# Attention with a top-32 cut and a max-out MLP: a first sweep over seven groups of keys, and half of the masks split between VectorE and GpSimd

## The chip, the cores and the metric

The kernel runs on one core of a Trainium2 chip. What counts is the time of one execution on the device in microseconds (us): the median of several runs. Five engines work side by side, each with a queue of its own that is taken in order: TensorE (PE, with its weight loads shown apart as PEld), VectorE (DVE), ScalarE (ACT), GpSimd (POOL) and SyncE (SP), which here issues most of the transfers.

## What is computed

Eight batches of eight heads, 576 tokens, head size 64. Of each row of scores only the 32 largest are kept; the softmax runs over these. The heads' outputs go through an MLP whose hidden layer is the largest of three products. All is float32.

```python
scores = scale * np.matmul(q, k.transpose(0, 1, 3, 2))
kth = np.partition(scores, -top_k, axis=-1)[..., -top_k:-top_k + 1]   # top_k = 32
scores = np.where(scores >= kth, scores, -1000000000.0)
scores = scores - np.max(scores, axis=-1, keepdims=True)
attn = np.exp(scores)
attn = attn / (np.sum(attn, axis=-1, keepdims=True) + 1e-09)
out = np.matmul(attn, v)
...
h = np.maximum(np.maximum(x @ w1, x @ w2), x @ w3)     # x: 4608 x 512, h: 4608 x 768
return h @ w_out
```

## The kernel before

**Tiles and units.** A tile is 128 queries of one head against all 576 keys. A unit is two or four tiles of a pair of heads; 288 tiles in 80 units. For each unit these steps run, and the letters are the names that the program gives to them:

- `q` (PE): scores into PSUM; `e` (ACT, `evac`): evacuation, scaled, into `ssb`.
- `s` (DVE, `sweep`): the first sweep. A MAX8 instruction finds the eight largest of each of eight groups of 72 keys and puts them into `L`.
- `N` (ACT, `negate`), `p1` to `p5` (DVE, `pivot`): from the four largest of each group (`nA`, negated) and the next four, the 24th largest of all of these is found: the pivot, a lower bound. MATCH_REPLACE8 and MAX8 pick the smallest 16 of the 32 negated values, which one instruction compares with the sorted rest.
- `g` (ACT, `sign`): the sign of pivot minus score, and its sum, which tells the pivot's rank. `w` (POOL, `window`): sign times score. `k` (DVE, `below`): a MAX8 over that row gives the eight values under the pivot. `h` 0 to 2 (DVE, `pick`): the 32nd largest, `kth`, from these nine and the rank.
- `m` (DVE, `mask`): one instruction with two tensor inputs turns the scores below `kth` into 1 minus score and the others into minus score, in place, and counts the former into `lost` by its accumulator. Since the scores are tiny (scaled by 2^-61), the exponential that follows makes 0 of the former. `x` (ACT, `expo`): the exponential and its sum.
- `T`, `E` (PE, ACT): transposes and their copies; `v` (PE): the product with the values; `y`, `Y`, `Z` (DVE, ACT, POOL): the result is scaled and split into two f16 halves `xh` and `xl`.

**The MLP.** Per batch there are two spans of tokens, 256 and 320 wide; for each, hidden-layer products on PE (L706, f16, three per pair of halves), evacuation and maximum (ACT L713, DVE L715), a split into halves (ACT L718, POOL L721), and then the second layer (L766) and the output. In the first 200 us the weights are also loaded, decoded on DVE (L253 to L255), scaled and cut into halves.

**What sets the order.** All steps are written down as `Piece`s: an engine, a cost in ns, what it needs and which buffers it takes. `in_order` then plays a list schedule: of each engine's pieces that lie within a window of ranks (`place_of` of the unit plus an entry of the table `OFFSETS`) it takes the first that can start, with a patience per engine, and so writes out each engine's queue before the kernel runs. The MLP's pieces are `fill`: on PE they are taken where no attention piece can start sooner. Pieces marked `alone` (the mask among them) are not put beside a POOL piece: they wait in the schedule for POOL to be free, and POOL's wait for them. On the chip the queues run in that order, and an instruction waits for what it needs.

Of the kernel before, what the change touches and what calls it, by code (L numbers as in the profile page):

```python
# [8 lines left out]
F32 = mybir.dt.float32  # L9
F32R = mybir.dt.float32r  # L10
F16 = mybir.dt.float16
# [9 lines left out]
G = 8  # L21
GW = 72
# [12 lines left out]
LEAD = 122.6  # L35
# [29 lines left out]
def in_order(pieces, fill):  # L65
# [35 lines left out]
    while left:  # L101
# [32 lines left out]
NSM = 2
LOAD_QK = 4000
DECODES = 2
DECODE_IN = 1920.0
DECODE_OUT = 1920.0
LOAD_JOB = 6500
SCORES = 960  # L140
PATIENCE = {'PE': 83.0, 'DVE': 164.4, 'ACT': 0.0, 'POOL': 81.9, 'SP': 0.0}


@with_exitstack
def kernel(ctx, tc, q, k, v, moe_w1, moe_w2, moe_w3, moe_w_out, out):
    nc = tc.nc
    B, NP, _, S = q.shape
    H, D = 2 * NP, q.shape[2] // 2
    P = 128
# [153 lines left out]
    def cut(j, part):  # L303
# [8 lines left out]
        def scaled():  # L312
            down = scale_of[f"w{j}"][0] if j < 3 * NB else scale_of["rows"][:, (j - 3 * NB) * P // CUT:(j - 3 * NB) * P // CUT + 1]
            box["ws"] = io.tile([P, 2 * CUT], F32, name="ws", bufs=2).rearrange("p (c n) -> p c n", n=CUT)
            nc.scalar.activation(box["ws"], w, AF.Copy, scale=down)

        def high():
            nc.scalar.copy(hi, box["ws"])  # L318

        def low():  # L320
            nc.gpsimd.tensor_tensor(lo, box["ws"], hi, ALU.subtract)
        return scaled, high, low

    pieces, fill = [], []
    rings = {nm: Ring(k) for nm, k in dict(s=2, tr=2, m=2, ssb=NSSB, L=NSM, nA=NSM, n8=NSM, nb=3, w=NWB, oh=2, pm=PMB, rs=3, sums=3, den=3,
                                           rsw=2, pT=1, xs=2, junk=2, books=2, vt=6, x=2, h1=3, ob=2, ws=2, qk=3).items()}

    def piece(engine, cost, run, needs=(), rank=(0.0, None), takes=(), mode=None, alone=False):
        x = Piece(engine, cost, run, needs, rank, [(rings[r], rel) for r, rel in takes], mode, alone)
        pieces.append(x)  # L330
        return x

    def scale_pieces(parts_, needs, rank):
        a = piece("DVE", 63, parts_[0], needs, rank)
        rel = []
# [755 lines left out]
```

## Time and profile before

| | before |
|---|---|
| median of 3 runs | 1258.01 us (1257.69 to 1258.57) |
| the profiled execution | 1259.42 us, its span 1257.6 us |
| PE busy | 1146.8 us, 91% |
| DVE busy | 1146.7 us, 91% |
| ACT busy | 1038.8 us, 83% |
| POOL busy | 569.3 us, 45% |

The span is the time from the first to the last instruction of the profiled execution. Busy time counts every moment in which an engine has at least one instruction under way; matmuls overlap in their pipeline and their ends are modelled, so their mean duration is longer than the step from one to the next, and the same holds for short DVE instructions. The view of the slices cuts the span into 40 equal parts of 31.4 us. A view by stretches gives for each engine the busy time and, in brackets, how many instructions started there.

### The profile page before, as it was taken

How to read it: one execution, taken by the hardware profiler on the slowest of the kernel's cores; microseconds unless marked ns; L12 is line 12 of the kernel's file. 1: busy time of each engine (PE TensorE's matmuls, PEld its weight loads, DVE VectorE, ACT ScalarE, POOL GpSimd, SP SyncE). 2: the span in 40 equal slices, each digit the busy share in tenths (PEclk: the TensorE clock that was granted, in tenths of full speed). 3: DMA queues.
4: the chain of work that ended last, by engine and by line, in shares of the span. 5: the costliest groups of instructions: out<-in, count | busy, mean ns of one | idle time of the engine just before them, and what ended most of it. 6: DMA issues, size and time to landing. Idle time of an engine off the chain costs nothing.

```text
span 1257.6 us, 27583 instructions
## 1 busy us (share of the span) xinstructions
PE 1146.8 (91%) x8817; PEld 776.2 (62%) x8817; DVE 1146.7 (91%) x5728; ACT 1038.8 (83%) x2692; POOL 569.3 (45%) x503
## 2 busy tenths in 40 slices
PE   5275886999899999999999999999999999999998
PEld 2142653566576666766676666766677665767765
DVE  7999999999999999999999999999999999997121
ACT  6587888999989988999999989898899989897211
POOL 2444644654345544545555545445535454544111
PEclk8567986999999999999999999999999999999999
DMA  7141121202010102010101102020101000000000
GB/s 246 34 158 39 52 70 49 66 2 80 21 58 18 60 1 76 11 47 31 47 31 39 39 2 85 1 77 2 60 19 60 18 20 26 1 19 2 17 18 29
DMA packets 25754, 54.41 MB, mean 43 GB/s; under 512 B 2688, under 2 KB 2944, under 8 KB 25600
## 3 DMA queue, kind: packets, MB, share of 16 engines
q1 hardware_dynamic: 25296, 52.14, 12.6%
q8 instruction: 71, 1.16, 0.4%
q14 instruction: 83, 0.68, 0.2%
q10 hardware_dynamic: 304, 0.43, 0.1%
HBM read 43.12 MB, written 9.44 MB: 42 GB/s over the span
## 4 chain that ended last, share of the span: by engine, by line
DVE 49%; PE 39%; ACT 7%; issue 3%; POOL 1%; DMA 0%; ACTq 0%; DVEq 0%
PE m L706 19%; DVE L L478 13%; DVE ssb L565 9%; DVE Q L526 8%; PE m L766 5%; PE tr L625 5%; PE tr L650 5%; PE s L461 4%; DVE h L715 3%; DVE nR L502 2%; ACT w L517 2%; ACT pm L574 2%; DVE wall L254 1%; DVE n L504 1%; DVE n L496 1%
## 5 line engine op out<-in xcount | busy, mean ns | idle before, releaser
L522 POOL TENSOR_TENSOR w<-ssb,w 128x576 f32<-128x576 f32 x288 | 414.9, 1460 | 259.3 <-ACT w L517 257.0
L706 PE MATMUL m<-xh,wall 128*128 128x256 f16 (+1 forms) x2304 | 436.5, 287 | 4.8 <-DVE h L715 3.6
L706 PEld LDWEIGHTS <-wall 128*128 128x128 f16 x3456 | 338.0, 98 | 95.4 <-issue 15.9
L478 DVE MAX8 L<-ssb 128x8 f32<-128x72 f32 x2304 | 331.2, 218 | 6.8 <-ACT ssb L469 6.7
L706 PE MATMUL m<-xl,wall 128*128 128x320 f16 (+1 forms) x1152 | 330.7, 287 | 0.0
L574 ACT ACTIVATE pm<-ssb,nb 128x576 f32<-128x576 f32 x288 | 222.7, 775 | 42.4 <-DVE ssb L565 41.7
L565 DVE SCALAR_TENSOR_TENSOR ssb<-ssb,kth 128x576 f32<-128x576 f32 x288 | 241.7, 873 | 2.2
L517 ACT ACTIVATE w<-ssb,Q 128x576 f32<-128x576 f32 x288 | 223.2, 775 | 14.9 <-DVE Q L509 13.5
L633 ACT COPY pT<-tr 128x512 f32<-128x512 f32 (+1 forms) x432 | 215.1, 512 | 12.1 <-PE tr L622 6.6
L526 DVE MAX8 Q<-w 128x8 f32<-128x576 f32 x288 | 212.3, 747 | 1.3 <-POOL w L522 0.8
L625 PE MATMUL tr<-ident,pm 128*128 128x128 f32 x1152 | 183.0, 286 | 33.3 <-ACT pm L574 15.1
L461 PE MATMUL s<-qk 64*128 64x288 f32 (+1 forms) x1280 | 191.1, 451 | 16.6 <-ACT ssb L469 11.1
L469 ACT ACTIVATE ssb<-s 128x576 f32<-128x576 f32 x288 | 184.3, 650 | 10.0 <-PE s L461 9.7
L625 PEld LDWEIGHTS tr<-ident,pm 128*128 128x128 f32 x1152 | 130.2, 144 | 98.5 <-ACT pm L574 39.3
L650 PE MATMUL tr<-pT,vt 128*64 128x256 f32 (+1 forms) x1920 | 183.3, 340 | 0.1
L715 DVE SCALAR_TENSOR_TENSOR h<-m,rises,h 128x256 f32<-128x256 f32 (+1 forms) x192 | 97.2, 506 | 67.4 <-PE m L706 67.3
L650 PEld LDWEIGHTS tr<-pT,vt 128*64 128x64 f32 x1920 | 109.8, 140 | 69.1 <-issue 20.7
L721 POOL TENSOR_TENSOR hl<-h,hh 128x256 f16<-128x256 f32 (+1 forms) x96 | 72.7, 758 | 171.4 <-ACT hh L718 171.3
L461 PEld LDWEIGHTS s<-qk 64*128 64x128 f32 (+1 forms) x1280 | 99.9, 184 | 76.4 <-ACT ssb L469 28.2
L674 POOL TENSOR_TENSOR xl<-xs,xh 128x256 f16<-128x256 f32 (+1 forms) x80 | 55.1, 688 | 196.4 <-ACT xh L670 196.3
L766 PE MATMUL m<-wall,hh 128*128 128x512 f16 (+1 forms) x444 | 130.6, 377 | 3.2 <-ACT wall L318 1.2
L718 ACT CAST hh<-h 128x256 f16<-128x256 f32 (+1 forms) x96 | 41.5, 432 | 54.1 <-DVE h L715 53.4
(95 smaller groups left out, 1148.5 us busy)
## 6 DMA issues: line engine op xcount, KB each, us to landing
vt<-in_v_dram SPq DMA_DIRECT2D x32, 320.0 KB, 3.2
qk<-in_k_dram SPq DMA_DIRECT2D x34, 288.0 KB, 3.0
qk<-in_q_dram SPq DMA_DIRECT2D x33, 288.0 KB, 3.5
wall<-in_moe_w_dram SPq DMA_DIRECT2D x16, 512.0 KB, 6.0
out_dram<-ob SPq DMA_DIRECT2D x32, 256.0 KB, 2.0
wall<-in_moe_w_out_dram SPq DMA_DIRECT2D x3, 512.0 KB, 3.5
ssb<-in_moe_w_out_dram SPq DMA_DIRECT2D x3, 512.0 KB, 3.6
wall<-in_moe_w_dram SPq DMA_DIRECT2D x4, 256.0 KB, 5.9
```

Of the source, the lines that this page charges most:

```text
L461: nc.tensor.matmul(to[:, h, :HALF], both[sl, 0, c0:c0 + m], both[sl, 1, i * HALF:(i + 1) * HALF], start=True, stop=True)
L478: nc.vector.max(d["L"][:, t, k, :], d["ssb"][t][:, k * GW:(k + 1) * GW])
L517: nc.scalar.activation(d["w"][t], d["ssb"][t], AF.Sign, bias=d["Q"][:, t, 0:1], scale=-1.0, accum_out=d["cnt"][:, t:t + 1])
L522: nc.gpsimd.tensor_tensor(d["w"][t], d["ssb"][t], d["w"][t], ALU.mult)
L526: nc.vector.max(d["Q"][:, t, 1:NW], d["w"].pop(t))
L565: nc.vector.scalar_tensor_tensor(ss, ss, d["kth"][:, t:t + 1], ss, ALU.is_lt, ALU.subtract, accum_out=d["lost"][:, t:t + 1])
L574: nc.scalar.activation(d["pm", t // 2][:, t % 2], d["ssb"][t], AF.Exp, bias=d["nb"][:, t:t + 1], scale=-1.0 / SHRINK, accum_out=d["sums"][ ...
L625: nc.tensor.transpose(pt[:, j * P:(j + 1) * P], pm[:, i, 64 * i + j * P:64 * i + (j + 1) * P], ident)
L633: nc.scalar.copy(pT[:, 512 * i:512 * i + m] if i < 2 else pT[:, 8 * P:10 * P], pt[:, :m])
L650: nc.tensor.matmul(to, vt[:, block if i < 4 else 8 + h, :], keys, start=(i == 0), stop=(i == 4))
L706: nc.tensor.matmul(box["ps", i][:, :c1 - c0], a, bb[:, kc, c0:c1], start=(kc == 0 and k == 0), stop=(kc == KC - 1 and k == 2))
L766: nc.tensor.matmul(box["po"][:n, :ds.stop - ds.start], a[:, f, cs], columns_of(bb, ds), start=(f == 0 and k == 0), stop=(f == FC - 1 and k ...
```

## The change

The first sweep is cut into seven groups of 82 or 83 keys: three of them need only the first half of the scores, four the rest. What follows works on 28 values where it had 32, and the pivot is looked up among nine places instead of eight, so that it is again the 24th largest. Of each unit's tiles, numbers 1 and 3 get another mask: a comparison with one tensor input on DVE writes 1 or 0 as f16 into a new tile `under` (three buffers) and counts with the same accumulator; a subtraction on POOL then makes `under` minus score, in place in `ssb`. The exponential of such a tile needs the new POOL piece `M`. The planner's costs for the sweep halves and the masks, two of its patiences, its window of ranks and the whole table `OFFSETS` have new numbers.

```diff
-G = 8
-GW = 72
+G = 7
+EDGES = (0, 82, 164, 247, 329, 412, 494, 576)
+FRONT = 3
...
-LEAD = 122.6
+LEAD = 121.9
...
-OFFSETS = {'C0': -22.23, 'C1': -0.68, 'C2': 16.29, 'C3': 22.05, ...}
+OFFSETS = {'C0': -11.78, 'C1': 1.57, 'C2': 14.49, 'C3': 21.94, ...}
...
+SOFT = (1, 3)
+NM = 3
...
-PATIENCE = {'PE': 83.0, 'DVE': 164.4, 'ACT': 0.0, 'POOL': 81.9, 'SP': 0.0}
+PATIENCE = {'PE': 72.0, 'DVE': 163.8, 'ACT': 0.0, 'POOL': 104.8, 'SP': 0.0}
...
-            for k in range(i * G // 2, (i + 1) * G // 2):
-                nc.vector.max(d["L"][:, t, k, :], d["ssb"][t][:, k * GW:(k + 1) * GW])
+            for k in range(FRONT, G) if i else range(FRONT):
+                nc.vector.max(d["L"][:, t, k, :], d["ssb"][t][:, EDGES[k]:EDGES[k + 1]])
...
-            z = d["z"] = sm.tile([P, 4, 8], F32, name="z", bufs=2)
-            nc.vector.scalar_tensor_tensor(z[:, :nt], d["n8"][:, :nt, 1], -SHRINK, b9s[n % 3][:, :nt, 0:8], ALU.mult, ALU.min)
+            z = d["z"] = sm.tile([P, 4, 9], F32, name="z", bufs=2)
+            low = d["n8"].rearrange("p t a b -> p t (a b)")[:, :nt, 4 * G - 24:4 * G - 15]
+            nc.vector.scalar_tensor_tensor(z[:, :nt], low, -SHRINK, b9s[n % 3][:, :nt], ALU.mult, ALU.min)
...
-        nc.vector.scalar_tensor_tensor(ss, ss, d["kth"][:, t:t + 1], ss, ALU.is_lt, ALU.subtract,
-                                       accum_out=d["lost"][:, t:t + 1])
+        if t in SOFT:
+            m = d["under", t] = wk.tile([P, S], F16, name="under", bufs=NM)
+            nc.vector.tensor_scalar(m, ss, d["kth"][:, t:t + 1], None, ALU.is_lt, ALU.add, accum_out=d["lost"][:, t:t + 1])
+        else:
+            nc.vector.scalar_tensor_tensor(ss, ss, d["kth"][:, t:t + 1], ss, ALU.is_lt, ALU.subtract,
+                                           accum_out=d["lost"][:, t:t + 1])
+
+    def drop(n, t):
+        d = st[n]
+        ss = d["ssb"][t]
+        nc.gpsimd.tensor_tensor(ss, d.pop(("under", t)), ss, ALU.subtract)
...
-                p(("s", g, i), "DVE", 1080, lambda g=g, i=i: sweep(n, g, i),
+                p(("s", g, i), "DVE", 1170 if i else 890, lambda g=g, i=i: sweep(n, g, i),
...
-            p(("m", t), "DVE", 740, lambda t=t: mask(n, t), needs=[d["h", 2]], alone=True)
-            p(("x", t), "ACT", 770, lambda t=t: expo(n, t), needs=[d["m", t], d["p2"]] + ([d["x", t - 1]] if t else [last_x[0]] if last_x else []),
+            if t in SOFT:
+                p(("m", t), "DVE", 530, lambda t=t: mask(n, t), needs=[d["h", 2]], takes=[("under", held(n, "under", t))], alone=True)
+                p(("M", t), "POOL", 1430, lambda t=t: drop(n, t), needs=[d["m", t]])
+                held(n, "under", t).append(d["M", t])
+            else:
+                p(("m", t), "DVE", 800, lambda t=t: mask(n, t), needs=[d["h", 2]], alone=True)
+            p(("x", t), "ACT", 770, lambda t=t: expo(n, t), needs=[d["M" if t in SOFT else "m", t], d["p2"]] + ([d["x", t - 1]] if t else [last_x[0]] if last_x else []),
```

How this moves instructions is shown at three places. In the changed program the lines below the diff's first part stand some 13 further down: L565, the mask, is L573, the soft mask is L571, the subtraction L579, the sweep L481, the hidden-layer products L719.

On PE, just ahead of the first 128x320 product of the hidden layer (first batch, second span), before:

```order
L766 LDWEIGHTS hl
L766 MATMUL m<-wall,hl 128x512
L625 MATMUL tr<-ident,pm 128x128 x4
L461 MATMUL s<-qk 128x288 x4
L706 LDWEIGHTS wall
L706 MATMUL m<-xh,wall 128x320
```

And in the changed program:

```order
L779 LDWEIGHTS hl
L779 MATMUL m<-wall,hl 128x512
L464 MATMUL s<-qk 128x288 x4
L719 LDWEIGHTS wall
L719 MATMUL m<-xh,wall 128x320
```

It is the 680th row of PE's queue in both; one group of four transposes has moved behind this place.

On DVE, ahead of the first step on such a product (the last row of each), before:

```order
L565 SCALAR_TENSOR_TENSOR ssb,lost<-ssb,kth 128x576
L509 TENSOR_REDUCE Q<-z 128x4
L496 MAX n_2845<-nA 128x8 x2
L498 TENSOR_REDUCE nb<-nA 128x2
L502 MATCH_REPLACE nR<-n_2845,nA 128x32 x2
L504 MAX n_2845<-nR 128x8 x2
L478 MAX L<-ssb 128x8 x8
L177 TENSOR_SCALAR e_2887<-s_2883 128x1
L180 TENSOR_SCALAR down_v<-e_2887 128x1
L181 TENSOR_SCALAR back_v<-e_2887 128x1
L715 SCALAR_TENSOR_TENSOR h_2900<-m,rises,h_2831 128x320
```

And in the changed program:

```order
L571 TENSOR_SCALAR under,lost<-ssb,kth 128x576
L541 SCALAR_TENSOR_TENSOR oh<-spots,cnt 128x36
L513 TENSOR_REDUCE Q<-z 128x4
L481 MAX L<-ssb 128x8 x6
L180 TENSOR_SCALAR e_2785<-s_2779 128x1
L183 TENSOR_SCALAR down_v<-e_2785 128x1
L184 TENSOR_SCALAR back_v<-e_2785 128x1
L544 TENSOR_TENSOR oh<-oh,Q 128x36
L546 TENSOR_REDUCE kth<-oh 128x4
L571 TENSOR_SCALAR under,lost<-ssb,kth 128x576
L481 MAX L<-ssb 128x8 x8
L728 SCALAR_TENSOR_TENSOR h_2829<-m,rises,h_2761 128x320
```

Counted over the whole queue up to there: 51 tiles swept and 44 masked before; 50 swept, 20 masked and 21 with the soft mask after. A soft mask is now written ahead of the full masks of its unit.

On POOL, at the start of the fourth batch's MLP (the products of the 256-wide span are split, `hl` 128x256), before:

```order
L721 TENSOR_TENSOR hl<-h_9265,hh 128x256
L522 TENSOR_TENSOR w<-ssb,w 128x576 x4
L721 TENSOR_TENSOR hl<-h_9403,hh 128x256
L674 TENSOR_TENSOR xl<-xs,xh 128x256
L522 TENSOR_TENSOR w<-ssb,w 128x576 x2
L721 TENSOR_TENSOR hl<-h_9547,hh 128x256
```

And in the changed program:

```order
L734 TENSOR_TENSOR hl<-h_9215,hh 128x256
L526 TENSOR_TENSOR w<-ssb,w 128x576 x2
L734 TENSOR_TENSOR hl<-h_9298,hh 128x256
L579 TENSOR_TENSOR ssb<-under,ssb 128x576
L687 TENSOR_TENSOR xl<-xs,xh 128x256
L579 TENSOR_TENSOR ssb<-under,ssb 128x576 x2
L734 TENSOR_TENSOR hl<-h_9459,hh 128x256
```

The subtractions stand between the window products and the splits, in the one queue that POOL has.

## Rows read from the trace of the kernel before

**Rows 1.** The page's busy time of each engine, share of the span, instructions.

```profile
PE 1146.8 (91%) x8817; PEld 776.2 (62%) x8817; DVE 1146.7 (91%) x5728; ACT 1038.8 (83%) x2692; POOL 569.3 (45%) x503
```

**Rows 2.** The page's slices: busy tenths of PE and DVE in 40 equal parts.

```profile
PE   5275886999899999999999999999999999999998
...
DVE  7999999999999999999999999999999999997121
```

**Rows 3.** Busy time by stretches: from:to and length, then each engine, PE's clock, transfers.

```profile
0.00:238.00 238.00, 155.15 (x968) 92.94 (x969) 225.28 (x1018) 183.45 (x436) 109.04 (x92) 0.78 0.28 91
238.00:1163.00 925.00, 902.99 (x7214) 620.98 (x7213) 905.79 (x4677) 837.00 (x2221) 449.48 (x396) 1.00 0.10 33
1163.00:1258.00 95.00, 88.64 (x639) 62.25 (x637) 15.59 (x34) 18.32 (x37) 10.77 (x15) 0.99 0.06 21
```

**Rows 4.** Waits of PE, 0 to 238 us: us in total, times, longest.

```profile
PE tr L622 <- ACT rsw L594: 9.9, 6, 3.5
PE s L461 <- ACT ssb L469: 9.0, 7, 2.8
```

**Rows 5.** Waits of PE, 238 to 1163 us.

```profile
PE tr L625 <- ACT pm L574: 7.4, 19, 0.8
PE tr L625 <- DVE xs L667: 4.5, 6, 1.6
```

**Rows 6.** Stretches, the hidden layer's products (L706) alone: PE, PEld, clock, transfers.

```profile
600.00:650.00 50.00, 19.61 (x154) 14.77 (x153) 1.00 0.15 49
...
1150.00:1200.00 50.00, 36.67 (x302) 29.39 (x301) 1.00 0.03 11
```

**Rows 7.** DVE's groups: xcount | busy us, mean ns | idle before, releaser.

```profile
L565 DVE SCALAR_TENSOR_TENSOR ssb<-ssb,kth 128x576 f32<-128x576 f32 x288 | 241.7, 873 | 2.2
L526 DVE MAX8 Q<-w 128x8 f32<-128x576 f32 x288 | 212.3, 747 | 1.3 <-POOL w L522 0.8
L478 DVE MAX8 L<-ssb 128x8 f32<-128x72 f32 x2304 | 331.2, 218 | 6.8 <-ACT ssb L469 6.7
```

**Rows 8.** DVE in order of time, 19 to 26 us: start, duration.

```profile
19.96 1.16 DVE L478 MAX8 L<-ssb 128x8 f32<-128x72 f32 x8
...
23.91 0.82 DVE L565 SCALAR_TENSOR_TENSOR ssb<-ssb,kth 128x576 f32<-128x576 f32 x1
24.65 0.08 DVE L565 DVE_READ_ACCUMULATOR ssb<-ssb,kth 128x1 f32 x1
24.65 0.81 DVE L565 SCALAR_TENSOR_TENSOR ssb<-ssb,kth 128x576 f32<-128x576 f32 x1
25.39 0.08 DVE L565 DVE_READ_ACCUMULATOR ssb<-ssb,kth 128x1 f32 x1
```

**Rows 9.** DVE in order of time, 42 to 43 us: a piece of weights is decoded.

```profile
42.27 0.41 DVE L253 TENSOR_SCALAR wall<-wall 128x512 int32<-128x512 int32 x1
42.71 0.69 DVE L254 SCALAR_TENSOR_TENSOR wall<-wall 128x512 int32<-128x512 int32 x1
```

**Rows 10.** All masks (shortest/median/longest ns), then one in time, and POOL beside it.

```profile
L565 DVE SCALAR_TENSOR_TENSOR ssb<-ssb,kth x288: 792/816/2017, 23.9 to 1152.1; 128x576 f32<-128x576 f32 x144
...
1146.44 1.27 DVE L565 SCALAR_TENSOR_TENSOR ssb<-ssb,kth 128x576 f32<-128x576 f32 x1
...
1144.24 2.86 POOL L522 TENSOR_TENSOR w<-ssb,w 128x576 f32<-128x576 f32 x2 [0.40 <-ACT w L517]
```

**Rows 11.** POOL's window products: shortest/median/longest ns, first and last start.

```profile
L522 POOL TENSOR_TENSOR w<-ssb,w x288: 1396/1412/2034, 16.3 to 1145.7; 128x576 f32<-128x576 f32 x144
```

**Rows 12.** PE in order of time: last 256-wide product, first 320-wide one, last attention product.

```profile
166.91 0.27 PE L706 MATMUL m<-xl,wall 128*128 128x256 f16 x1
...
237.52 0.45 PE L706 MATMUL m<-xh,wall 128*128 128x320 f16 x2
...
1160.91 1.39 PE L650 MATMUL tr<-pT,vt 128*64 128x64 f32 x40
```

**Rows 13.** ACT's exponentials, as a group.

```profile
L574 ACT ACTIVATE pm<-ssb,nb 128x576 f32<-128x576 f32 x288 | 222.7, 775 | 42.4 <-DVE ssb L565 41.7
```

More of the change, by code (lines that the diff above doesn't have):

```diff
@@ new lines @@
+OFFSETS = {'C0': -11.78, 'C1': 1.57, 'C2': 14.49, 'C3': 21.94, 'D0': -0.89, 'D1': 1.37, 'D2': 12.64, 'D3': 21.59, 'E00': 1.24, 'E01': 4.19, 'E02': 7.06, 'E10': 2.48, 'E11': -9.39, 'E12': -10.72, 'M1': 2.32, 'M3': 0.2, 'N': -1.36, 'Pl': 15.24, 'R': -4.16, 'S': -1.04, 'T00': -31.31, 'T01': 1.87, 'T02': -5.16, 'T10': -27.81, 'T11': -74.59, 'T12': -31.2, 'U': -3.52, 'U0': -84.53, 'V': -20.01, 'V0': -4.99, 'Y': 5.89, 'Z': -35.06, '_E00': -9.99, '_E01': -16.43, '_E02': 12.21, '_E10': -13.49, '_E11': 3.11, '_E12': -75.26, '_M1': -25.94, '_M3': -38.0, '_N': 4.19, '_Pl': -68.46, '_T00': -89.36, '_T01': -53.02, '_T02': -61.38, '_T10': -87.71, '_T11': -45.9, '_T12': -44.92, '_Y': -90.44, '_Z': 5.66, '_d0': 8.47, '_d1': 3.91, '_e00': -104.08, '_e01': -55.38, '_e10': 2.42, '_e11': -93.97, '_g0': -79.61, '_g1': -27.89, '_g2': -52.22, '_g3': -68.68, '_h0': 4.32, '_h1': 5.91, '_h2': -6.96, '_k0': -1.07, '_k1': 4.2, '_k2': -1.61, '_k3': -65.96, '_m0': -94.49, '_m1': -59.45, '_m2': -47.72, '_m3': -2.87, '_p1': 3.02, '_p2': 5.92, '_p3': 5.81, '_p4': -62.98, '_p5': 3.13, '_q0': 2.91, '_q1': 3.31, '_r0': -103.87, '_r1': 2.85, '_s00': 2.28, '_s01': 4.22, '_s10': 5.6, '_s11': 5.03, '_v': -7.06, '_w0': 4.4, '_w1': 15.54, '_w2': -99.3, '_w3': -86.28, '_x0': 4.41, '_x1': 10.93, '_x2': 10.66, '_x3': 11.92, '_y': -53.47, '_z0': 7.36, '_z1': 9.82, 'd0': 10.18, 'd1': -22.01, 'e00': -2.4, 'e01': -0.92, 'e10': 7.32, 'e11': 6.42, 'g0': 1.79, 'g1': -19.63, 'g2': 0.53, 'g3': -7.96, 'h0': 4.89, 'h1': 7.68, 'h2': -0.45, 'k0': 1.46, 'k1': -16.24, 'k2': 0.82, 'k3': -17.67, 'm0': -11.24, 'm1': -11.56, 'm2': 3.55, 'm3': 4.7, 'p1': 8.93, 'p2': 6.67, 'p3': -14.32, 'p4': -9.89, 'p5': 7.5, 'q0': -0.51, 'q1': 1.19, 'r0': 1.01, 'r1': -10.21, 's00': 6.99, 's01': 5.11, 's10': 3.2, 's11': 6.27, 'v': 12.48, 'w0': -19.99, 'w1': 17.43, 'w2': -92.23, 'w3': -30.77, 'x0': 11.19, 'x1': 13.44, 'x2': 7.43, 'x3': 5.71, 'y': -11.83, 'z0': 4.21, 'z1': 3.23}
@@ L325 @@
     rings = {nm: Ring(k) for nm, k in dict(s=2, tr=2, m=2, ssb=NSSB, L=NSM, nA=NSM, n8=NSM, nb=3, w=NWB, oh=2, pm=PMB, rs=3, sums=3, den=3,
-                                           rsw=2, pT=1, xs=2, junk=2, books=2, vt=6, x=2, h1=3, ob=2, ws=2, qk=3).items()}
+                                           rsw=2, pT=1, xs=2, junk=2, books=2, vt=6, x=2, under=NM, h1=3, ob=2, ws=2, qk=3).items()}
     def piece(engine, cost, run, needs=(), rank=(0.0, None), takes=(), mode=None, alone=False):
@@ L1029 @@
                         mask(i, t)
+                        if t in SOFT:
+                            drop(i, t)
                         expo(i, t)
```

1 line of the change is left out of this document (removed).

## The prediction

> **What bounds the kernel now.** I read the busy shares first, then the slices, then one table by stretches. TensorE (PE) and VectorE (DVE) are each busy 91% of the span, ScalarE (ACT) 83%, GpSimd (POOL) 45% [rows 1]. The slices show that the two leaders are not full at the same times: DVE is at 9 from the second slice to the 36th, PE only from the eighth on, with a few 8s [rows 2]. So I cut the span at two places: where the wide hidden-layer products (128x320) of the first batch start on PE, 237.5 us, and where PE's last attention product ends, about 1162 us [rows 12].
>
> - From 0 to 238 us DVE is busy 225.3 us and PE 155.2: PE idles 83 us, DVE sets the pace [rows 3]. PE waits there for ACT, for instance 9.0 us for evacuated scores and 9.9 us for the widened row sums [rows 4], and ACT waits in its turn for what DVE sweeps and masks.
> - From 238 to 1163 us PE is busy 903.0 of 925 us and DVE 905.8: both nearly full, PE idle 22 us [rows 3]. PE's largest waits are 7.4 us for the exponentials and 4.5 us for the scaled x [rows 5].
> - From 1163 us on PE does nothing but MLP products, 95 us of them; DVE is busy for 15.6 us [rows 3].
>
> Is PE in the middle really at its peak, or stretched by its pipeline? In the last stretch, where nothing else is left, 302 hidden-layer products took 36.67 us, 121 ns each; at 600 us, between attention work, 154 took 19.61 us, 127 ns each [rows 6]. The shape mix differs a little between the two, so 5% is the most that hides there. I take PE as full. The MLP is filler: a batch's products can be run any time after its attention, and the 95 us at the end are what has piled up (by the order, the rest of the seventh batch and all of the eighth). An attention that ends earlier with a full PE only moves filler from the middle to the end. **The time can therefore shrink by PE's idle time and by little else**: 83 us before 238, 22 us after.
>
> **The change, part by part.**
>
> *Sweep over seven groups.* Eight MAX8 over 72 columns take 1.16 us [rows 8], one alone 218 ns [rows 7], so the step from one to the next is (1.16 - 0.218) / 7 = 0.135 us. A MAX8 over 576 columns takes 747 ns [rows 7], so a column costs (747 - 218) / 504 = 1.05 ns. Seven groups of 82.3 columns step by 0.135 + 10.3 x 1.05 ns = 0.146 us. Per tile of 128 rows: 8 x 0.135 - 7 x 0.146 = 0.058 us; 288 tiles: 16.7 us of DVE. The small instructions behind it (three MAX8 and one MATCH_REPLACE8 per tile) work on 28 columns in place of 32: 4 x 4 x 1.05 ns x 288 = 4.8 us. The pivot's comparison has nine places per tile in place of eight, four more columns in 64 of its 80 instructions, some 0.3 us: nothing.
>
> *Half of the masks.* A mask now starts every 0.74 us, accumulator read included [rows 8]. The soft mask (a comparison with one tensor input, f16 out, the same accumulator) is not in this trace. Its bounds: below, the nearest one-tensor instruction, the shift and mask over 512 columns, takes 0.41 us, while the two-tensor instruction of the same size behind it takes 0.69 [rows 9]; 0.41 is my lower end with everything else hidden. Above, 0.74, as if nothing were won. I take 0.50, which is 0.41 x 576 / 512 plus half of the 0.08 us accumulator read, because the instruction is nearer in kind to that row. 144 x (0.74 - 0.50) = 34.6 us of DVE, between 0 and 47.5.
>
> *GpSimd.* The subtraction is a two-tensor instruction of the shape of the window product, 1.41 us [rows 11]: 144 x 1.41 = 203 us more, 569 + 203 = 772 us, 61% of the span. POOL stays far from being the bound. Its cover is not free, though. Mask 1146.44 lasted 1.27 us while a window product ran from 1144.24 to 1147.10 [rows 10]: DVE's two-tensor instructions stand still while POOL works. The mean of a mask is 873 ns, its median 816 [rows 7, 10]: 57 ns x 288 = 16.4 us lost to this now. With POOL busy 772 / 569 = 1.36 times as long I add 6 us, and up to 16 at the upper end.
>
> *DVE in sum:* 16.7 + 4.8 + 34.6 - 6 = 50 us less.
>
> *What of it reaches the end, first stretch.* In the order, PE comes to the first 128x320 product at the same point in both programs, with the same products ahead of it but for one group of four transposes, which now comes later. In DVE's order ahead of the first 128x320 step stand 51 swept tiles and 44 masks before; 50 swept tiles, 20 full and 21 soft masks after. Sweep: 51 x 1.080 - 50 x 1.022 = 4.0. Masks: 44 x 0.74 - 20 x 0.74 - 21 x 0.50 = 7.3. Small ones: 50 x 17 ns = 0.9. Sum 12.2 us, and DVE sets the pace there, so PE gets to this place **12 us** earlier. (The first narrow products come later in DVE's order, behind two more weight pieces and five more swept tiles, but from 167 to 237.5 us PE has no hidden-layer product to do [rows 12], and this hides it.)
>
> *Second stretch.* PE must still do its 903 us. With DVE relieved by about 38 us more in it, the waits for exponentials and scaled x should shrink. The 22 us cannot all go: some are handed on by ACT (837.0 of 925 us busy [rows 3]), some will be new waits for POOL. I take half, **10 us**. *Third stretch:* unchanged.
>
> Span: 1257.6 - 12 - 10 = 1235.6. The profiled execution took 1259.42, 1.8 more than its span; it lies 1.4 above the median of the runs, 1258.0. On the median's scale: 1258.0 - 22 = **1236 us**.
>
> **The rivals.**
>
> 1. *The full mask's pace.* If the accumulator keeps the soft mask at the pace of the full one, 0.74 us, the change gives DVE 21.5 us instead of 56, and POOL's work is wasted. First stretch: 4.0 + 0.9 + 3 masks fewer x 0.74 = 7; second: DVE stays about as full as PE, 3. Time 1258 - 10 = 1248. For it: no row has a one-tensor instruction with an accumulator. Against it: 0.41 against 0.69 us in [rows 9]. The Trainium skill, "SBUF — State Buffer", section "Who interferes with whom", says that a tensor_scalar may use both ports of VectorE, but not in the form that also writes out its accumulator; by that rule this rival is the forecast. No run here shows it yet.
>
> 2. *DVE's gain goes through in full.* If PE's 903 us are stretched by waits that do not show, all 50 us come off: 1208. For it: PE's weight loads are busy for only 621 of those 925 us, 67%. Against it: in the last stretch, at full pace, they are busy 62.25 of 95 us, 66% [rows 3]. The Trainium skill, "Trainium Kernel Development and Optimization", section "Performance Expectations", calls matmul busy time a bad measure and the busy share of the weight loads a good one; by it PE would have room, and the trace speaks against that here.
>
> 3. *The lock eats it.* If each of the 41 masks and the small two-tensor instructions ahead of 238 us waits 0.25 us longer for a POOL now fuller, 41 x 0.25 = 10 us of the first 12 are gone, and the second stretch keeps its 22 us: 1256, no change that counts.
>
> 4. *Slower: ACT waits for POOL.* An exponential of a soft tile now needs DVE 0.50 and then POOL 1.41 us, 1.17 more than the 0.74 of a full mask, and POOL takes it in order, behind window products that themselves wait for ACT. Behind an exponential that waits stand on ACT the score evacuations and the copies that feed PE. In the second stretch ACT has 925 - 837 = 88 us to spare [rows 3], and over the span it waits 41.7 us for masks already [rows 13]. With 144 - 21 = 123 soft tiles there, the gain of the whole change is gone once the wait not covered exceeds (88 + 22) / 123 = 0.89 us per soft tile. At the full 1.17 it is 1.17 x 123 - 88 = 56 us on top of 1236, that is 1292; since PE's filler hides a part, I put the case between the two, at 1275. Against it: in the order the soft masks are placed ahead of the full ones of their tiles or early, so that POOL has time.
>
> **How the numbers follow.** Forecast (1236, by itself 1226 to 1246) 56%; rival 1 (1248) 11%; rival 2 (1208) 7%; rival 3 (1256) 10%; rival 4 (1275) 16%. A measurement of this kernel can tell about 0.2%, 2.5 us, from no change. Faster: 56 + 11 + 7 = 74%; same: 10%; slower: 16%. The range leaves out rival 4 and the lower half of rival 2: 1214 to 1257; the unknown costs (soft mask from 0.41 to 0.74, lock up to 16 us) lie within.
>
> **What would show it right or wrong.** Right: the first 128x320 product on PE at about 225 us; PE idle some 70 us before it and 10 to 15 between it and the end of attention; the last stretch again 95 us or less; DVE less than 96% busy in the middle; the soft mask near 0.5 us. Wrong: a soft mask at 0.7 us (rival 1); masks with a mean far over 0.9 us (rival 3); a wait of ACT's exponentials for POOL's subtraction of over 100 us in sum, with PE waiting for exponentials (rival 4); a PE busy time clearly under 1140 us (rival 2).

## The result, and the profile after

| | before | after |
|---|---|---|
| median of the runs | 1258.2 us | 1266.08 us (1262.89 to 1267.91) |
| ratio, 95% interval | | 1.0061 [1.0044, 1.0077] |
| span of the profiled execution | 1257.6 us | 1266.0 us |

Slower by 0.6%. The forecast of 1236 us and its range, 1214 to 1257, both missed, and on the wrong side.

The page's busy times of the changed kernel, against [rows 1]: DVE is busy 8 us less, not 50; PE is as before; POOL is busy 196 us more, where 203 were counted.

```profile
PE 1145.2 (90%) x8817; PEld 774.8 (61%) x8817; DVE 1138.6 (90%) x5440; ACT 1036.0 (82%) x2692; POOL 765.4 (60%) x647
```

By stretches (from:to and length, then busy time and started instructions of PE, PEld, DVE, ACT, POOL, PE's clock, transfers), against [rows 3]:

```profile
0.00:238.00 238.00, 146.75 (x933) 88.35 (x934) 223.66 (x935) 177.91 (x423) 132.62 (x109) 0.78 0.27 91
238.00:1163.00 925.00, 901.10 (x7150) 617.50 (x7149) 893.23 (x4457) 831.59 (x2213) 617.65 (x519) 1.00 0.10 33
1163.00:1266.00 103.00, 97.39 (x738) 68.93 (x736) 21.74 (x51) 26.51 (x59) 15.14 (x20) 0.99 0.06 20
```

The two places at which the prediction cut the span, PE in order of time (start, duration): the first wide product comes at 240.1 instead of 237.5 us, the last attention product ends at 1177.6 instead of 1162.3 [rows 12].

```profile
240.10 0.45 PE L719 MATMUL m<-xh,wall 128*128 128x320 f16 x2
...
1176.21 1.39 PE L663 MATMUL tr<-pT,vt 128*64 128x64 f32 x40
```

So the first stretch is 2.6 us longer, the second 12.7, and the third 6.9 shorter (48 of the MLP's products, 6.5 us of PE, stood behind the last attention product in the order and now stand ahead of it): 8.4 us of span.

DVE's and POOL's groups that the change touches (xcount | busy us, mean ns | idle before, releaser), against [rows 7]:

```profile
L481 DVE MAX8 L<-ssb 128x8 f32<-128x82 f32 (+1 forms) x2016 | 314.5, 228 | 5.7 <-ACT ssb L472 5.7
...
L530 DVE MAX8 Q<-w 128x8 f32<-128x576 f32 x288 | 214.3, 750 | 12.5 <-POOL w L526 11.5
L579 POOL TENSOR_TENSOR ssb<-under,ssb 128x576 f32<-128x576 f16 x144 | 204.2, 1418 | 229.3 <-DVE under L571 174.0 <-DVE oh L541 22.0 <-DVE Q L513 15.6
...
L573 DVE SCALAR_TENSOR_TENSOR ssb<-ssb,kth 128x576 f32<-128x576 f32 x144 | 132.7, 926 | 0.3
...
L571 DVE TENSOR_SCALAR_CACHE_REDUCE under<-ssb,kth 128x576 f16<-128x576 f32 x144 | 115.9, 805 | 1.9
```

The sweep gave what was worked out (331.2 to 314.5 us). The soft mask gave nothing: 805 ns, where a full mask that nothing holds up takes 812. The third thing is new: DVE idles 11.5 us ahead of the window's MAX8, waiting for POOL, where it idled 0.8.

To put sizes on this I split DVE's time in each kernel: for each line and form of its instructions the step from its start to the next start, without the idle time in it, is taken at its 20th percentile; this is the undisturbed step. What the other steps are longer is time held up; the rest is idle. Stretches end at each kernel's own first wide product and own last attention product; the idle time behind DVE's last instruction in a stretch, 2 to 4 us in the second, is left out. The split is an estimate.

| us: undisturbed / held up / idle | first stretch | second stretch |
|---|---|---|
| before | 201.3 / 23.7 / 12.7 | 857.0 / 48.7 / 17.3 |
| after | 194.0 / 31.8 / 14.4 | 845.5 / 52.6 / 35.5 |
| e1, seven groups alone | 197.8 / 28.8 / 12.3 | 839.9 / 43.5 / 20.2 |
| e2, after with all masks full | 193.4 / 25.8 / 15.2 | 846.6 / 56.5 / 37.2 |
| e4, after without the count | 188.5 / 33.5 / 14.2 | 808.9 / 51.9 / 46.4 |

Undisturbed work fell by 7.3 + 11.5 = 18.8 us, near the 21.5 that sweep and small instructions were to give (between 17 and 23 if the instructions are grouped in other ways). Held-up time rose by 12.0 and idle time by 19.9, and these two ate more than that.

### The profile page after: what moved, and what is told of

Its sections match the earlier page's. It is cut to its first block, busy times and chain, and to the rows that moved or that the text cites. A ratio compares the mean times of both kernels' runs of the same rounds, so it can differ in the third digit from the quotient of the medians.

```text
span 1266.0 us, 27534 instructions
## 1 busy us (share of the span) xinstructions
PE 1145.2 (90%) x8817; PEld 774.8 (61%) x8817; DVE 1138.6 (90%) x5440; ACT 1036.0 (82%) x2692; POOL 765.4 (60%) x647
## 4 chain that ended last, share of the span: by engine, by line
DVE 37%; PE 34%; ACT 11%; POOL 3%; issue 3%; DVEq 0%; POOLq 0%; ACTq 0%
PE m L719 14%; DVE L L481 8%; DVE Q L530 7%; PE m L779 5%; PE tr L663 5%; PE s L464 4%; DVE under L571 4%; PE tr L638 4%; DVE ssb L573 4%; ACT w L521 4%; DVE h L728 3%; POOL w L526 2%; ACT pm L587 2%; DVE nR L505 2%; ACT pT L646 2%
## 5 line engine op out<-in xcount | busy, mean ns | idle before, releaser
L526 POOL TENSOR_TENSOR w<-ssb,w 128x576 f32<-128x576 f32 x288 | 409.0, 1441 | 60.2 <-ACT w L521 57.1
L719 PE MATMUL m<-xh,wall 128*128 128x256 f16 (+1 forms) x2304 | 434.0, 286 | 5.3 <-DVE h L728 4.7
L719 PEld LDWEIGHTS <-wall 128*128 128x128 f16 x3456 | 336.9, 98 | 91.4 <-issue 14.7
L579 POOL TENSOR_TENSOR ssb<-under,ssb 128x576 f32<-128x576 f16 x144 | 204.2, 1418 | 229.3 <-DVE under L571 174.0
L719 PE MATMUL m<-xl,wall 128*128 128x320 f16 (+1 forms) x1152 | 329.4, 286 | 0.4 <-POOL xl L687 0.4
L481 DVE MAX8 L<-ssb 128x8 f32<-128x82 f32 (+1 forms) x2016 | 314.5, 228 | 5.7 <-ACT ssb L472 5.7
L530 DVE MAX8 Q<-w 128x8 f32<-128x576 f32 x288 | 214.3, 750 | 12.5 <-POOL w L526 11.5
L464 PE MATMUL s<-qk 64*128 64x288 f32 (+1 forms) x1280 | 194.3, 455 | 19.8 <-ACT ssb L472 14.6
L472 ACT ACTIVATE ssb<-s 128x576 f32<-128x576 f32 x288 | 184.2, 650 | 12.1 <-PE s L464 11.5
L663 PE MATMUL tr<-pT,vt 128*64 128x256 f32 (+1 forms) x1920 | 187.0, 345 | 3.3 <-ACT pT L646 3.3
L573 DVE SCALAR_TENSOR_TENSOR ssb<-ssb,kth 128x576 f32<-128x576 f32 x144 | 132.7, 926 | 0.3
L571 DVE TENSOR_SCALAR_CACHE_REDUCE under<-ssb,kth 128x576 f16<-128x576 f32 x144 | 115.9, 805 | 1.9
```

What stands on the lines that cost most here:

```text
L464: nc.tensor.matmul(to[:, h, :HALF], both[sl, 0, c0:c0 + m], both[sl, 1, i * HALF:(i + 1) * HALF], start=True, stop=True)
L481: nc.vector.max(d["L"][:, t, k, :], d["ssb"][t][:, EDGES[k]:EDGES[k + 1]])
L526: nc.gpsimd.tensor_tensor(d["w"][t], d["ssb"][t], d["w"][t], ALU.mult)
L530: nc.vector.max(d["Q"][:, t, 1:NW], d["w"].pop(t))
L579: nc.gpsimd.tensor_tensor(ss, d.pop(("under", t)), ss, ALU.subtract)
L663: nc.tensor.matmul(to, vt[:, block if i < 4 else 8 + h, :], keys, start=(i == 0), stop=(i == 4))
```

## The experiments

### What the accumulator costs: e4, and two more pairs

In the changed kernel's own order, the count is taken out of the soft mask. This is for measuring only: from the counts the kernel also sees whether the cut that it found is the 32nd largest score, and does all over where it is not.

```diff
+            nc.vector.memset(books[b][2], float(S - TOPK))
...
-            nc.vector.tensor_scalar(m, ss, d["kth"][:, t:t + 1], None, ALU.is_lt, ALU.add, accum_out=d["lost"][:, t:t + 1])
+            nc.vector.tensor_scalar(m, ss, d["kth"][:, t:t + 1], None, ALU.is_lt)
```

> The changed kernel in its own order, but the soft mask does not write out its accumulator; the count of scores under the cut in these tiles is left out (a constant of 544 stands for it, set once per batch). Price: without the accumulator the comparison should take 0.35 to 0.45 us, about half; if it stays near 0.7 us, the accumulator is not what keeps it slow. Theory (my chain was right but for the price of the soft mask): 144 x 0.33 = 47 us less on DVE, 1232 to 1242. Rival (POOL's lock eats it, the comparison now holds the shared port too): 1255 to 1265, with masks and soft masks whose mean is 0.15 us or more over their median.

Measured: 1239.39 us, 0.9857 [0.9842, 0.9873], against 1.0061 with the count. DVE in order of time, the first unit, in the changed kernel and then in e4 (start, duration):

```profile
23.00 0.81 DVE L571 TENSOR_SCALAR_CACHE_REDUCE under<-ssb,kth 128x576 f16<-128x576 f32 x1
23.73 0.08 DVE L571 DVE_READ_ACCUMULATOR under<-ssb,kth 128x1 f32 x1
23.73 0.81 DVE L573 SCALAR_TENSOR_TENSOR ssb<-ssb,kth 128x576 f32<-128x576 f32 x1
```

```profile
23.00 0.52 DVE L572 TENSOR_SCALAR under<-ssb,kth 128x576 f16<-128x576 f32 x1
23.43 0.81 DVE L574 SCALAR_TENSOR_TENSOR ssb<-ssb,kth 128x576 f32<-128x576 f32 x1
```

From the soft mask's start to the next instruction's it is 0.73 us with the accumulator, the pace of a full mask, and 0.43 without. The summaries (shortest/median/longest ns) of the soft masks and of the full ones in the changed kernel, and of the soft ones in e4:

```profile
L571 DVE TENSOR_SCALAR_CACHE_REDUCE under<-ssb,kth x144: 787/807/816, 23.0 to 1163.1; 128x576 f16<-128x576 f32 x144
```

```profile
L573 DVE SCALAR_TENSOR_TENSOR ssb<-ssb,kth x144: 789/812/2015, 22.3 to 1164.4; 128x576 f32<-128x576 f32 x144
```

```profile
L572 DVE TENSOR_SCALAR under<-ssb,kth x144: 479/520/1731, 23.0 to 1132.7; 128x576 f16<-128x576 f32 x144
```

The other end of these lines tells something too: without the count the fast form is sometimes held up to 1731 ns, beside a POOL that is busy 62% of the time; with it none of 144 takes over 816, among full masks that take up to 2015. This is no matter of where they stand: in the changed kernel 53 of the 144 soft masks overlap in time with an instruction on POOL, 21 of them by over 0.7 us. Of its 31 full masks with such an overlap 23 take over 900 ns.

One pair could be an accident of one order, so it was repeated in the orders of e14 and e15 (below).

> The order of e14 (1277.6 us), soft masks without accumulator, as e4 has it in the order of the changed kernel; the counts of lost entries for tiles 1 and 3 are left out (a constant stands in their place). It asks whether e4's 26.7 us belong to the accumulator or to that one order. If 34 us of DVE are what counts, 1247 to 1257 here, as far below e14 as e4 is below the changed kernel. If e4's time was its order's, 1262 to 1278.

> The same in the order of e15 (1284.0 us), with the counts for tiles 1 and 3 left out again. If 34 us of DVE are what counts, 1253 to 1263. If e4's time was its order's, 1268 to 1284.

| order of | with the count | without | difference | DVE busy, with and without |
|---|---|---|---|---|
| the changed kernel | 1266.08 | 1239.39 (e4) | -26.7 | 1138.6, 1097.6 |
| e14 | 1277.55 | 1248.21 (e18) | -29.3 | 1141.6, 1103.1 |
| e15 | 1283.96 | 1252.08 (e20) | -31.9 | 1141.1, 1099.6 |

Within each pair every engine has the same order. Three times the same: some 40 us of DVE's busy time, placed on 144 masks, are worth 27 to 32 us of time (26 to 34 by the ratios; e18 has 0.9921, e20 0.9953). By stretches, e4:

```profile
0.00:236.00 236.00, 151.65 (x944) 90.69 (x944) 221.75 (x928) 179.02 (x426) 134.87 (x111) 0.78 0.28 92
236.00:1147.00 911.00, 900.99 (x7280) 630.13 (x7278) 860.99 (x4344) 835.96 (x2233) 626.94 (x523) 1.00 0.10 34
```

The last attention product in e4:

```profile
1145.83 1.39 PE L664 MATMUL tr<-pT,vt 128*64 128x64 f32 x40
```

The attention ends at 1147.2 instead of 1177.6 us. PE, which looked full, let it happen: its sum of busy time over the whole span fell from 1145.2 to 1135.7 us for the same products, and its idle time by 21.

### The two halves of the change apart: e1, e3, e9, e2

e1 is the kernel before with only the seven groups (sweep and pivot), the planner's costs, table and the masks left as they were.

```diff
-G = 8
-GW = 72
+G = 7
+EDGES = (0, 82, 164, 247, 329, 412, 494, 576)
+FRONT = 3
```

> The kernel before with the seven groups alone: all masks full, the planner's costs and offsets as before, so every queue has the order of before. DVE loses some 16 to 21 us of work, POOL gets none. Theory 1 (DVE's work paces the first 238 us, PE the rest): 5 us off the first stretch and 2 to 5 after it, 1248 to 1251 us. Rival (DVE paces the whole attention): 1238 to 1242. Rival (the old order holds the engines to its own pace, a shorter sweep only makes DVE wait): 1255 to 1259.

Measured: 1241.73 us, 0.9877 [0.9862, 0.9892]. This lies in the range for a DVE that paces the whole attention, and not in that of my theory. The kernel still does all of the work that the reference asks for, and it is faster than both kernels.

e3 is the other half alone: the kernel before, eight groups, its own table, with soft masks on tiles 1 and 3 and the subtraction written right behind each, of which the planner knows nothing.

```diff
+        if t in SOFT:
+            m = d["under", t] = wk.tile([P, S], F16, name="under", bufs=NM)
+            nc.vector.tensor_scalar(m, ss, d["kth"][:, t:t + 1], None, ALU.is_lt, ALU.add, accum_out=d["lost"][:, t:t + 1])
+            nc.gpsimd.tensor_tensor(ss, m, ss, ALU.subtract)
```

> The kernel before with eight groups and its own order, but tiles 1 and 3 get the soft mask and, written right behind it, POOL's subtraction, which the planner does not know of. DVE's undisturbed work is unchanged within 2 us. Theory (POOL's load costs): 1264 to 1275, since to 16 us of lock and late window products comes a later exponential. Rival (POOL's work is free, only the order matters): 1256 to 1260.

Measured: 1351.58 us, 1.0750 [1.0736, 1.0765], far above both ranges. Its waits in the second stretch (who waits for whom: us, times, longest):

```profile
ACT pm L581 <- POOL ssb L570: 74.5, 62, 2.6
POOL w L524 <- ACT w L519: 59.7, 54, 2.7
PE tr L632 <- ACT pm L581: 48.1, 53, 2.2
DVE Q L528 <- POOL w L524: 38.8, 44, 2.0
```

This is the mechanism of rival 4: POOL takes a subtraction in order behind window products that wait for ACT, ACT's exponential waits for the subtraction, PE for the exponential. In the changed kernel the planner has placed the pieces so that it hardly occurs; who waits there for the subtraction:

```profile
L579 POOL TENSOR_TENSOR ssb<-under,ssb x144: 1277/1291/1907, 24.0 to 1164.0; 128x576 f32<-128x576 f16 x144
...
  ACT pm L587: 3.0, 10
```

e9 and e2 keep the changed kernel's table and seven groups, and make all masks full. In e9 the planner knows that (all masks booked at 800 ns, no subtraction). In e2 the plan and so the order are the changed kernel's (soft mask 530, subtraction 1430 on POOL), while on the chip full masks run and no subtraction.

```diff
-SOFT = (1, 3)
+SOFT = ()
```

```diff
-        if t in SOFT:
-            m = d["under", t] = wk.tile([P, S], F16, name="under", bufs=NM)
...
-        nc.gpsimd.tensor_tensor(ss, d.pop(("under", t)), ss, ALU.subtract)
+        d.pop(("under", t), None)
```

> The changed kernel without soft masks: seven groups and the new table, patiences and window, all masks full and booked at 800 ns, no subtraction on POOL, in plan or on the chip. DVE's work is that of the seven groups with the old table (1241.7). Theory (the price is the fault, not the table): 1240 to 1250. Rival (the new table makes a poorer order whatever the masks are): 1260 to 1275.

> The changed kernel in its own order, but tiles 1 and 3 get the full mask on DVE and the 144 subtractions on POOL are left out; the result stays the same. DVE's work is the same as in the changed kernel if a soft mask costs as much as a full one (0.74 us). Theory (POOL's 204 us more cost by the lock on DVE and by late window products): 1248 to 1254, DVE's excess over its undisturbed steps falls from 63 to below 55 us. Rival (the price of the soft mask, 0.2 us over the plan, is all, POOL costs nothing): 1263 to 1267. Rival (the new order alone is worse): 1260 or more, with PE idle before the wide products of the first batch still over 88 us.

Measured: e9 1246.17 us, 0.9901 [0.9872, 0.9930]; e2 1267.98 us, 1.0083 [1.0070, 1.0097]. The same instructions, 22 us apart, by order alone. In e2 more full masks stand beside POOL's work: 37 of 288 take over 900 ns, in e9 18, and what they take over their median is 23 us in sum against 12. The rest of the 22 us is not traced to an instruction here. And e2 is as slow as the changed kernel, against my theory that POOL's work costs: at this order the whole exchange, 144 soft masks and 204 us on POOL for 144 full masks, changes next to nothing. In the table above it costs 6 us of held-up time in the first stretch and gives about as much back in the second. DVE's new wait in the second stretch, in the changed kernel and in e2:

```profile
DVE Q L530 <- POOL w L526: 11.5, 15, 1.9
```

```profile
DVE Q L530 <- POOL w L526: 10.4, 13, 1.9
```

POOL has no subtraction to do in e2, and DVE waits the same. So the wait comes with the order, not with the subtraction's work.

### Is PE what paces the second stretch? e10

The kernel before without the third of the hidden layer's products (high half of the weights by low half of x), which is left out:

```diff
-                for k, (a, bb) in enumerate(((high, xh), (low, xh), (high, xl))):
+                for k, (a, bb) in enumerate(((high, xh), (low, xh))):
```

> The kernel before, in its own order, with the third of the three hidden-layer products (the low half of x) left out: the result lacks that part. PE loses about a third of 466 us, some 150 us, of which 25 in the last stretch. My prediction's claim (PE is full from 238 us on and sets the pace): the end of attention moves from 1162 to 1145 or earlier, as far as DVE lets it, and the time to 1215 or less. Rival (DVE sets the pace of the middle too, PE's filler only uses gaps): attention ends at 1155 to 1163, and the time falls by the last stretch alone, to 1225 to 1235.

Measured: 1234.94 us, 0.9812 [0.9796, 0.9828]. By stretches:

```profile
0.00:238.00 238.00, 148.01 (x895) 86.38 (x896) 224.73 (x1018) 183.82 (x436) 109.31 (x92) 0.78 0.28 91
238.00:1163.00 925.00, 827.11 (x6331) 528.94 (x6330) 905.55 (x4681) 835.85 (x2224) 450.74 (x398) 1.00 0.10 33
1163.00:1234.00 71.00, 64.11 (x443) 43.04 (x440) 14.15 (x30) 16.48 (x33) 9.73 (x14) 0.97 0.08 28
```

PE lost 107.6 us of work, most of it in the middle, and the attention ended only 4 us sooner (1158.2):

```profile
1156.82 1.39 PE L650 MATMUL tr<-pT,vt 128*64 128x64 f32 x40
```

DVE is busy there for 905.55 us as before [rows 3]. Of the 24 us of span that were gained, 20 came off the last stretch, where PE is alone. Up to 1163 us DVE and what it waits for set the pace, and PE's filler fits beside it. The order plays no part in this: without the 1152 products left out, PE's order is that of the kernel before, and so are those of ACT, POOL and, but for its last 42 rows, DVE.

### What in the order costs 22 us: prices, the listed subtraction, or accident

Five kernels change numbers of the plan. e5 is the changed kernel with the soft mask booked at what it takes (740 in place of 530). e12 is the order of e5 with full masks and no subtraction on the chip. e7 is e1 with the masks of tiles 1 and 3 booked at 530, e11 is e9 with the same: a wrong price without a subtraction in the plan. e13 is e2 with the masks booked at 800 and the subtraction at 1 ns.

e5 (e12 has it too, with e2's edit), then e7 (and so e11, from 800):

```diff
-                p(("m", t), "DVE", 530, lambda t=t: mask(n, t), needs=[d["h", 2]], takes=[("under", held(n, "under", t))], alone=True)
+                p(("m", t), "DVE", 740, lambda t=t: mask(n, t), needs=[d["h", 2]], takes=[("under", held(n, "under", t))], alone=True)
```

```diff
-            p(("m", t), "DVE", 740, lambda t=t: mask(n, t), needs=[d["h", 2]], alone=True)
+            p(("m", t), "DVE", 530 if t in (1, 3) else 740, lambda t=t: mask(n, t), needs=[d["h", 2]], alone=True)
```

> The changed kernel with one number changed: the planner books 740 ns for a soft mask, what the trace of the changed kernel shows for it, in place of 530. The work is the same, the lists are made anew, with the same table of offsets. Theory (the order is made for a soft mask of 0.53 us and runs out of step with one of 0.74): part of the 8 us comes back, 1246 to 1258. Rival (a table of offsets fits only the costs that it was made with, so that any other price makes it worse): 1264 to 1285.

> The order of e5 (soft mask booked at 740, the subtraction still listed at 1430), with full masks and without the subtraction on GpSimd's part of the chip: the difference to e5 (1279.1 us) is the work on GpSimd alone. If GpSimd's 204 us of subtractions held e5 up, 1250 to 1258. If the order held it up, 1272 to 1283.

> Seven groups, all masks full, old table (1241.7 us with the old order), but the planner books 530 ns in place of 740 for the masks of tiles 1 and 3, which still take 0.74: the wrong price alone, with no soft mask and nothing on POOL. Theory (a price 0.21 us too low puts the order out of step): 1252 to 1270, DVE's idle time from the wide products to the end of attention rises from 20 to 30 us or more. Rival (the price hardly matters): 1239 to 1248.

> The changed kernel with all masks full and no subtraction on GpSimd (e9, 1246.2 us), with the masks of tiles 1 and 3 booked at 530 instead of 800. If the wrong price alone makes the 22 us between e2 and e9, 1263 to 1273. If the place that the subtraction takes in the planner's list of GpSimd makes them, 1243 to 1250, since no such piece is listed here.

> The changed kernel with full masks booked at 800 and the subtraction listed at 1 ns and not executed: between e2 (530 and 1430, 1268.0 us) and e9 (800 and no such piece, 1246.2 us). If the 1430 ns that the planner gives GpSimd for the subtraction push the exponentials back, 1243 to 1252 here. If the list is disturbed by anything that differs from the costs for which its offsets were found, the time can be anything between 1246 and 1280.

Five more ask how much a new listing does by itself. e6 books e1's two sweeps at 890 and 1170, nearer to what they take; e16 books them at 1070 in place of 1080; e17 books e1's mask at 750 in place of 740; e14 is the changed kernel with 540 for 530, e15 with 1400 for 1430. The edit of e15, for all of them:

```diff
-                p(("M", t), "POOL", 1430, lambda t=t: drop(n, t), needs=[d["m", t]])
+                p(("M", t), "POOL", 1400, lambda t=t: drop(n, t), needs=[d["m", t]])
```

A change of 10 ns (30 in e15) in one cost leaves each engine the same instructions and re-sorts them for most of the program: DVE's order differs from its 80th of 5440 rows on in e16, from its 549th in e15, in e14 and e17 in between.

> The kernel before with seven groups and the old table (e1, 1241.7 us), with only the planner's costs of the two sweeps changed from 1080 each to 890 and 1170, which is nearer to what three and four MAX8 take. DVE's work is that of e1 to the instruction; only the order can differ. If a re-listed order of a given table is worth little when the costs are right, 1238 to 1246. If a table is worth what it is only with the very costs that it was found with, and any re-listing spoils it, some 1255 to 1275, as for e7 (one price wrong, 1274).

> Seven groups alone (e1, 1241.7 us) with both sweeps booked at 1070 in place of 1080: the same instructions in an order that differs nearly from the start. If seven groups are worth their DVE time whatever the order, 1238 to 1246. If the order of e1 was a lucky or a preserved one, 1250 to 1275.

> Seven groups alone (e1) with the mask booked at 750 in place of 740; the order is that of e1 for the first 218 rows on DVE and differs behind. If seven groups are worth their DVE time whatever the order, 1238 to 1246. If the order of e1 was a lucky or a preserved one, 1250 to 1275.

> The changed kernel (1266.1 us) with the soft mask's price in the planner 540 in place of 530: the same instructions, nothing truer about the plan, but the list is made anew and the order differs from there on. If what a price says is what counts, 1264 to 1269. If any new listing of a table found for other numbers costs about what e6 and e7 cost (18 and 33 us), 1275 to 1300.

> The changed kernel with the subtraction on GpSimd booked at 1400 in place of 1430, otherwise as it is. If what a price says is what counts, 1263 to 1269. If the table is tied to its very numbers, 1275 to 1300; and if a new listing can as well go the other way, 1245 to 1262.

All kernels with seven groups whose masks take 0.73 us or more on DVE, by what their plan holds:

| plan | kernel: time, ratio with interval |
|---|---|
| all masks priced about right, no subtraction that takes time | e1 1241.7, 0.9877 [0.9862, 0.9892]; e13 1242.1, 0.9890 [0.9874, 0.9907]; e9 1246.2, 0.9901 [0.9872, 0.9930]; e16 1249.5, 0.9936 [0.9919, 0.9952]; e17 1253.0, 0.9969 [0.9957, 0.9982]; e6 1259.7, 1.0022 [1.0011, 1.0033] |
| subtraction listed at 1400 or 1430, soft mask at 530 or 540 | after 1266.1, 1.0061 [1.0044, 1.0077]; e2 1268.0, 1.0083 [1.0070, 1.0097]; e14 1277.6, 1.0162 [1.0145, 1.0179]; e15 1284.0, 1.0220 [1.0203, 1.0237] |
| subtraction listed at 1430, soft mask at 740 | e12 1271.1, 1.0123 [1.0107, 1.0140]; e5 1279.1, 1.0169 [1.0152, 1.0186] |
| no subtraction, two masks at 530 | e7 1274.3, 1.0133 [1.0116, 1.0150]; e11 1286.7, 1.0247 [1.0230, 1.0264] |

What follows, and what does not:

- A re-sorting that changes no work moves the time by up to 18 us (e1, e16, e17, e6; and after, e14, e15). No single pair with a smaller difference says anything on a price; the 8 us between the kernel before and the changed kernel are smaller too. In both families the kernel that keeps the numbers that its table came with (e1; after) is the fastest. e14, e15, e6 and e17 came out as "any new listing costs" had it, e16 just short of it.
- Still, the six kernels planned for full masks (0.988 to 1.002) and the eight planned for soft ones, in six orders (1.006 to 1.025), do not overlap. Between their means (0.9933 and 1.0150) lie 27 us. As far as these few orders tell, they are the price of planning for a soft mask, whether or not soft masks then run: e2, e12, e7 and e11 run full masks only.
- The wrong price is enough for that by itself (e7, e11: 33 and 40 us over e1 and e9, the latter above both ranges expected), but correcting it does not take the cost away while the subtraction stands in the plan (e5, e12; a new listing by itself cost e14 and e15 about as much). My expectation of e5, that the right price would bring the time back, fell. With the price right and the subtraction listed as nothing (e13), it is gone.
- The subtraction's work on the chip is 6 us between e12 and e5 by their ratios, and nothing between e2 and after.
- What in the plan makes the listed subtraction dear stays open. A mask piece is not put beside a POOL piece in the plan, so 206 us more of POOL leave fewer places for masks; that would fit e13 and e5, but it is argued, and was not tried. How the table would fare if it were made anew for the measured 0.73 us was not tried either.

## Why the prediction was wrong, point by point

- **PE is full in the middle, so only its idle time can go: failed.** e10 takes a tenth of PE's work away and the attention ends 4 us sooner; e4, with DVE relieved in the same order, ends it 30 us sooner. The pace of 127 against 121 ns [rows 6] could not show it: the second of these windows begins 12 us before the attention ends, and behind that end the same trace gives 116 ns (1163 to 1200 us) and 134 ns (1200 to 1250). A PE that takes filler whenever it has nothing else looks full at whatever speed the others go. The bound was the queue that was full of work that cannot be moved: DVE, 905.8 of 925 us [rows 3]. The 10 us for the second stretch were therefore sized by the wrong engine. This hurt both ways: of what DVE gained, 65 to 78% reached the end (27 to 32 of some 40 us in the three pairs, 16 of 21 in e1), so DVE's waits cost as well. Rival 2 (1208) had this mechanism, with a DVE gain that did not come.
- **Soft mask at 0.50 us, 34.6 us in sum: failed.** It steps by 0.73, next to the upper bound of the range given, and the term is 1.4 us. This is the failed step that decides the sign: without the accumulator the mask steps by 0.43 and the kernel takes 1239.4 us, where 1236 was forecast. (That the two are so near is in part luck: 0.43 is less than the 0.50 assumed.) The accumulator costs more than its read; it changes the pace of the whole instruction. The Trainium skill, "SBUF — State Buffer", section "Who interferes with whom", says that a tensor_scalar which also writes out its accumulator does not enter the mode that uses the port shared with GpSimd; the two summaries above (816 ns at most with it, up to 1731 without) agree.
- **Rival 1 (1248) was the right mechanism at the wrong price.** It gave the missing 35 us of DVE a price of 12 us of time; three pairs measured 27 to 32 for some 40. And neither it nor the forecast had a term for an order listed for a soft mask.
- **Sweep and small instructions, 21.5 us of DVE: right** (18.8 measured as undisturbed work, with the sweep's 16.7 exact). Alone it is worth 16.2 us in one order (e1), and between 16 and -3 over four (the eight groups' own order was not varied).
- **POOL +203 us: right in size** (204.2 for the subtractions, 196 for POOL as a whole). Luck is in it: in the median a subtraction takes 1291 ns, and those that are held up bring the mean to 1418. **Held-up time +6, up to 16: the size is within** (12.0), **the cause is not shown:** e2, without any subtraction, has 9.9 of the 12.0, so most of it came with the order and not with a busier POOL.
- **First stretch 12 us earlier: failed**, 2.6 us later. 5 of the 12 were the soft mask's. The products ahead of the first wide one were not quite the same either: by the trace three groups of four transposes and four score products fewer stand there, not one group of four. Undisturbed work fell by 7.3 us, and the hold-ups rose by 8.1, of which 6.0 are gone in e2 (rival 3's mechanism, here). Two of DVE's instructions that decode weights, before 238 us, in the kernel before, in the changed kernel, and in e2, which has the same order and no subtraction:

```profile
L255 DVE SCALAR_TENSOR_TENSOR wall<-wall 128x512 int32<-128x512 int32 x21 | 19.8, 943 | 0.7
L254 DVE SCALAR_TENSOR_TENSOR wall<-wall 128x512 int32<-128x512 int32 x21 | 17.3, 825 | 0.7
```

```profile
L257 DVE SCALAR_TENSOR_TENSOR wall<-wall 128x512 int32<-128x512 int32 x21 | 21.5, 1023 | 0.7
...
L258 DVE SCALAR_TENSOR_TENSOR wall<-wall 128x512 int32<-128x512 int32 x21 | 20.1, 957 | 0.7
```

```profile
L258 DVE SCALAR_TENSOR_TENSOR wall<-wall 128x512 int32<-128x512 int32 x21 | 18.4, 877 | 0.7
L257 DVE SCALAR_TENSOR_TENSOR wall<-wall 128x512 int32<-128x512 int32 x21 | 17.7, 841 | 0.7
```

  L257 answers to L254 of before, L258 to L255. Without the subtraction L257 takes 841 ns, near the 825 of before, and with it 1023: POOL's work falls on them, and e2 reaches its first wide product at 234.2 us.
- **Rival 4 (ACT waits for POOL): right sign, wrong mechanism.** The wait is 3.0 us in the changed kernel. It is real where the order does not provide for it (e3), and the price of providing for it was in no term. DVE's idle time rose with the new order from 17.3 to 35.5 us in the second stretch (37.2 in e2, without a subtraction). By the same split e9, with the new table and nothing listed for POOL, has 30.4, so what is listed for POOL accounts for the smaller part of the rise.
- **Third stretch unchanged: off by 6.9 us**, moved from the tail to ahead of the last attention product by the order; the two stretches together are 5.8 us longer.

## What to carry to other kernels

An engine that is kept busy by filler need not be the bound; look for the busy engine whose work cannot be put off, and test it by taking work away from each of the two. Price an instruction in the very form that it will have: an accumulator on a one-tensor comparison added 0.30 us to 0.43. Where the table of a schedule was found for given costs, a new listing can move the time by more than a change is worth, so judge a change over several orders. Truer costs in an old table are no remedy by themselves: e5 and e6 were slower with them.

## What the runs showed of the hardware that was not expected

- A comparison of 128x576 with one f32 tensor input and f16 result steps by 0.73 us with an accumulator and 0.43 us without. With it, it was never held up beside a busy POOL (787 to 816 ns over 144 of them, 53 of which overlapped with POOL's work), while full masks in the same program took up to 2015 ns.
- POOL's subtraction with one f16 input took 1291 ns in the median, the product of two f32 tensors of the same shape 1412 [rows 11]. Whether the type or the operation makes the difference was not tried.
- PE's busy time for the same 8817 matmuls in the same order is no constant: 1145.2 us in the changed kernel, 1135.7 in e4.
